# Reordering the second batch of a fused attention and MLP kernel: loads of k, q, v and the weights, and the order of up units and head pairs

## The chip, the cores and the metric

The kernel runs on one core of one Trainium2 chip. The metric is the device time of one execution in microseconds (us), smaller is better; a time is given as a median over several runs. The core has five engines, each working through its own list of instructions in order: TensorE (PE; PEld are its weight loads), VectorE (DVE), ScalarE (ACT), GpSimd (POOL) and SyncE (SP). TensorE writes into PSUM banks; the other engines read them. Transfers between the chip's main memory and the on-chip memory run on 16 DMA engines; here SP issues most of them (a hardware queue), and POOL issues those that also convert float32 to bfloat16 (a software queue).

## What is computed

Attention with a sliding window of 128 and a distance bias, 8 batches, 8 heads, 576 tokens, head size 64; its output, as 4608 tokens of 512, goes through an MLP with a hard-swish.

```python
def _attn_ref(q, k, v):
    B, H, S, D = q.shape
    scores = scale * np.matmul(q, k.transpose(0, 1, 3, 2))
    rel = pos[:, None] - pos[None, :]
    bias = slopes[:, None, None] * (-np.abs(rel).astype(np.float32))[None, :, :]
    mask = (rel >= 0) & (rel < 128)
    scores = np.where(mask, scores + bias[None], -1000000000.0)
    scores = scores - np.max(scores, axis=-1, keepdims=True)
    attn = np.exp(scores)
    attn = attn / (np.sum(attn, axis=-1, keepdims=True) + 1e-09)
    return np.matmul(attn, v).astype(np.float32)

def _moe_ref(x, w_in, w_out):          # x: 4608 x 512, w_in: 512 x 2048, w_out: 2048 x 512
    h = x @ w_in
    relu6 = np.clip(h + 3.0, 0.0, 6.0)
    g = h * relu6 / 6.0
    return (g @ w_out).astype(np.float32)
```

## The kernel before

**Tiling.** Attention works on pairs of heads: pair `g` has batch `g // 4` and heads `2 * (g % 4)` and the next, so batch 0 has pairs 0 to 3 and batch 1 pairs 4 to 7. The MLP works on tiles of 512 tokens, nine in all. One *up unit* (`moe_up`) is one block of 128 of the 2048 hidden columns for one tile of tokens: four matmuls of 512 columns (`up_mms`), then ACT's `r6` (line 524) and DVE's product (line 525) into `gbuf`. One *down step* (`moe_down`, lines 553 to 556) is four matmuls towards a block of 128 output rows. `units` holds all of these in their order, and `fill(n)` takes the next n of them; it stops before an up unit whose tokens are not attended yet (`done`).

**The order is written by hand.** The whole body stands under a manual schedule of all five engines, so each engine gets its instructions exactly in the order in which the Python code calls them. `first_batch` does the attention of batch 0, `second_batch` that of batch 1 among the 16 up units of token tile 0, and `segment` all the rest; the change touches `second_batch` and the last lines of `first_batch` ahead of `attend_split(0, ...)`.

**Steps of the second batch.**
- `load_double(b, dp, nm)` asks for k or q of four heads (two pairs, `dp` 0 or 1) in two loads of 288 KB into the left or right half of `ldbuf[1]` (k) or `ldbuf[0]` (q). `prepare_double` casts these to bfloat16 in two copies of 128 x 576 on the engines given (`P` POOL, `V` DVE). `wide_double` transposes the result with nine matmuls into a score bank and copies it, 128 x 1152, to `kTb` or `qTb` (line 290).
- `load_heads` and `load_block` ask for v (two heads at a time, and the last 64 tokens of all heads), `cast_heads` and `cast_v` turn these to bfloat16 on POOL (lines 199 and 196).
- `scores_diag(g)` and `scores_off(g)` are the score matmuls; each takes one of two score banks (`ps_sc`). `exp_diag(g, e)` is an exp on ACT and a select on POOL that masks it (line 388); `exp_off_full(g)` is one exp of 1024 columns (line 369).
- `attend(g)` multiplies with v (34 matmuls of 65 columns) into a score bank and normalises on DVE (lines 446 and 447). `back(g)` transposes the result (line 481) and ACT, for pair 7 DVE, copies it to `xT` (line 487).
- `up_begin` and `up_more` do an up unit of token tile 1 in parts, as that needs all four pairs of batch 1.
- `load_w_in(g)` and `load_w_out(g)` are POOL's converting loads of a quarter of the weights (512 columns of w_in, so up units 4g to 4g + 3, or 512 rows of w_out). The first quarter of w_in comes another way, through `load_raw` and `cast_raw`.
- `hold(buf, col)` writes one element of a load buffer on DVE: the load into that buffer that follows in the code has to wait for this write, and so is held back until DVE gets there.

**What sets the order of the transfers.** SP issues its loads in code order. Its completion counters are eight, used in turn, so at most eight of its loads are in flight: the ninth is issued when the first has landed. A load into a buffer waits until the casts that read the buffer's old contents are done.

Of the kernel before, what the change touches and what calls it, by code (L numbers as in the profile page):

```python
# [11 lines left out]
BF16 = mybir.dt.bfloat16  # L12
# [6 lines left out]
def kernel(  # L19
# [76 lines left out]
    def load_double(b, dp, nm, eng):  # L96
        for e in range(2):
            eng.dma_start(out=ldbuf["qk".index(nm)][:, ds((2 * dp + e) * RT * D, RT * D)],
                          in_=src_of[nm][b, ds(4 * dp, 4), :, :].rearrange(
                              "(i e) (a t) d -> e a i (t d)", e=2, t=RT)[e])  # L100
# [12 lines left out]
    def load_heads(b, nm, hp, eng):  # L113
        for e in range(2):
            h = 2 * hp + e
            eng.dma_start(out=tokens(b, nm)[:, 0:4, h, :],
                          in_=src_of[nm][b, h, 0:512, :].rearrange("(j p) d -> p j d", p=128))
# [57 lines left out]
    def load_w_in(g):  # L175
        nc.gpsimd.dma_start(
            out=w_in_sb[:, :, ts(g, 512)],
            in_=moe_w_in[:, ts(g, 512)].rearrange("(k p) f -> p k f", p=128))
# [15 lines left out]
    def cast_v(b, j, copy):  # L194
        n = min(128, S - j * 128)
        copy(out=vbuf[b % 2][:n, j, :, 0:D], in_=ld[b, "v"][:n, j, :, :])

    def cast_heads(b, hp, copy):
        copy(out=vbuf[b % 2][:, 0:4, ds(2 * hp, 2), 0:D], in_=ld[b, "v"][:, 0:4, ds(2 * hp, 2), :])
# [20 lines left out]
    st = {}  # L220
# [8 lines left out]
    def transposes(g, copies):  # L229
        b, hp = divmod(g, NP)  # L230
        for nm, dst, copy in (("q", qTb[b % 2], copies[0]), ("k", kTb[b % 2], copies[1])):
            src = st.pop((g, nm))
            tp = ps_h.tile([128, RT, RP], BF16, tag="h", name="tp", padded_shape=[128, 16, 64])
            for t in range(RT):
                for e in range(2):
                    r = slice(e * D, (e + 1) * D)
                    nc.tensor.transpose(tp[r, t, :], src[r, ts(t, D)], ident[r, r])
            copy(out=dst[:, hp, :, :].rearrange("p j c -> p (j c)")[:, 0:S].rearrange(
                "p (a t) -> p a t", t=RT), in_=tp.rearrange("p t a -> p a t"))

    def prepare_double(b, dp, copies, nms="kq", early=None):
        for nm, copy in zip(nms, copies):
            pr = prs.tile([128, RT, 2 * D], BF16, tag=f"pr{nm}", name="pr2")
            for e in range(2):
                copy(out=pr[:, :, ts(e, D)],  # L245
                     in_=ldbuf["qk".index(nm)][:, ds((2 * dp + e) * RT * D, RT * D)].rearrange(
                         "p (t d) -> p t d", t=RT))
                if early and (nm, e) == (nms[0], 0):
                    early()
            st[b, dp, nm] = pr  # L250
# [117 lines left out]
    def exp_off_full(g):  # L368
        nc.scalar.activation(out=st[g, "po"].rearrange("p e j c -> p e (j c)"),
                             in_=st[g, "sco"], func=ACT.Exp, scale=scale)  # L370
# [206 lines left out]
    def fill(n):  # L577
        for _ in range(n):
            if at[0] == len(units):
                return  # L580
            nt, fn, step = units[at[0]]
            if fn is moe_up and done[0] < NP * (min((nt * NT + NT - 1) // S, B - 1) + 1):
                return
            fn(nt if fn is moe_up else nt - 1, step)
            at[0] += 1
# [26 lines left out]
    def hold(buf, col):  # L612
        nc.vector.memset(ldbuf[buf][:, col:col + 1], 0.0)

    def first_batch():
        prepare(0, (V, A))
        warm_up(5)
        tables_diag(0)
        tables_off(0)
        transposes(0, (V, A))  # L620
        scores_diag(0)
        prepare(1, (P, V))
        nc.gpsimd.memset(ldbuf[2][:, 0:1], 0.0)
        load_heads(0, "v", 0, nc.sync)
        load_block(0, "v", 4, nc.sync)
        load_heads(0, "v", 1, nc.sync)
        load_heads(0, "v", 2, nc.sync)
        load_raw(0)
        load_raw(1)
        load_heads(0, "v", 3, nc.sync)  # L630
        load_raw(2)
        load_raw(3)
        transposes(1, (V, V))
        scores_off(0)
        exp_full(0)
        scores_diag(1)
        prepare_double(0, 1, (V, P), "qk")
        tables_off(1)
        scores_off(1)
        double_begin(0, 1, "q", ("av", "o"))  # L640
        double_begin(0, 1, "k", ("h", "h"))
        exp_full(1)
        double_copy(0, 1, "q", 0, (V, V))
        double_copy(0, 1, "k", 0, (A, A))
        tables_diag(2)
        tables_off(2)
        scores_diag(2)
        double_copy(0, 1, "q", 1, (V, V))
        double_copy(0, 1, "k", 1, (V, V))
        scores_off(2)  # L650
        exp_full(2)
        cast_heads(0, 0, P)
        cast_v(0, 4, P)
        cast_heads(0, 1, P)
        cast_heads(0, 2, P)
        load_w_in(1)
        cast_heads(0, 3, P)
        for ks in range(n_ks):
            cast_raw(ks, P)
        load_w_in(2)  # L660
        attend_split(0, ("av", "o"))
        scores_diag(3)
        attend_split(1, ("h", "h"))
        scores_off(3)
        exp_full(3)
        attend(2)
        hold(1, 0)
        for nm in "kq":
            load_double(1, 0, nm, nc.sync)
        back(0, "av")  # L670
        back(1, "o")
        attend(3)
        back(2, "h")
        up_begin(0, 0, 2)
        back(3, "av")
        up_begin(0, 1, 2, "o")
        up_more(0, 0, 3)
        up_more(0, 1, 3)
        done[0] = NP

    def second_batch():
        memsets_later()
        fill(5)
        hold(3, 0)
        load_heads(1, "v", 0, nc.sync)
        load_block(1, "v", 4, nc.sync)
        load_heads(1, "v", 1, nc.sync)
        for nm in "kq":
            load_double(1, 1, nm, nc.sync)
        for hp in (2, 3):  # L690
            load_heads(1, "v", hp, nc.sync)
        fill(2)
        prepare_double(1, 0, (P, V), "kq")
        load_w_in(3)
        fill(1)
        wide_double(1, 0, "k", V)
        wide_double(1, 0, "q", A)
        for dp in range(1):
            for nm in "kq":
                load_double(2, dp, nm, nc.sync)  # L700
        fill(2)
        g = NP
        scores_diag(g)
        exp_diag(g, 0)
        exp_diag(g, 1)
        fill(1)
        scores_off(g)
        exp_off_full(g)
        scores_diag(g + 1)
        exp_diag(g + 1, 0)  # L710
        exp_diag(g + 1, 1)
        fill(1)
        scores_off(g + 1)
        exp_off_full(g + 1)
        cast_heads(1, 0, P)
        cast_v(1, 4, P)
        cast_heads(1, 1, P)
        fill(1)
        attend(g)
        fill(1)  # L720
        attend(g + 1)
        back(g, "o")
        fill(1)
        prepare_double(1, 1, (P, V), "kq")
        back(g + 1, "o")
        wide_double(1, 1, "k", V)
        wide_double(1, 1, "q", A)
        for nm in "kq":
            load_double(2, 1, nm, nc.sync)
        fill(1)  # L730
        scores_diag(g + 2)
        exp_diag(g + 2, 0)
        exp_diag(g + 2, 1)
        load_w_out(0)
        up_begin(1, 0, 2)
        scores_off(g + 2)
        exp_off_full(g + 2)
        up_begin(1, 1, 2)
        scores(g + 3)
        exp_diag(g + 3, 0)  # L740
        exp_diag(g + 3, 1)
        exp_off_full(g + 3)
        cast_heads(1, 2, P)
        cast_heads(1, 3, P)
        load_w_out(1)
        prepare_double(2, 0, (P, P), "kq")
        load_w_out(2)
        load_w_out(3)
        attend(g + 2)
        attend(g + 3)  # L750
        prepare_double(2, 1, (P, P), "kq")
        nc.gpsimd.memset(ldbuf[2][:, 0:1], 0.0)
        load_tokens(2, "v")
        for dp in range(2):
            load_double(3, dp, "k", nc.sync)
        load_tokens(3, "q")
        back(g + 2)
        up_more(1, 0, 3)
        up_more(1, 1, 3)
        back(g + 3)  # L760
        done[0] = 2 * NP
        fill(4)
        double(2, 0, "k", 0, "av", A)
        fill(1)
        double(2, 0, "k", 1, "av", A)
        fill(1)
        wide_double(2, 0, "q", V)
        fill(4)
        scores_diag(2 * NP)
        scores_off(2 * NP)  # L770
# [94 lines left out]
```

## Time and profile before

| | us |
|---|---|
| median of three runs | 340.91 |
| lowest, highest | 339.87, 341.17 |
| the profiled execution | 340.78 |
| its span, first to last instruction | 339.1 |

| stretch (us) | what runs there |
|---|---|
| 0 to 20.9 | batch 0: constants, loads, attention |
| 20.9 to 27.7 | up units 0 to 7 of token tile 0 |
| 27.7 to 59.5 | batch 1's attention among up units 8 to 15 |
| 59.5 to 75.9 | up units of token tile 1, batch 2's transposes and first scores |
| 75.9 to 339 | down steps, up units and attention interleaved, to the end |

Landing times of loads in this profile, from issue: w_in's second, third and last quarter 8.3, 9.4 and 8.7 us; w_out's quarters 5.7, 5.4, 6.1 and 7.4; k and q of batch 1's first two pairs 4.4 to 7.7; of its second two pairs 4.9 to 5.5; its v 4.4 to 8.1.

A page of the profile has, among other parts, the busy time of each engine, the span in 40 slices with a digit for the busy share in tenths (8.48 us a slice here), and the clock that TensorE was granted. The timeline of an engine lists its instructions with their start and length, and in brackets how long the engine was idle before one and what ended that. In all of these L524 is line 524 of the kernel.

### The profile page before, as it was taken

What the parts mean: (1) busy time and instruction counts of PE and PEld (TensorE: products, weight loads), DVE (VectorE), ACT (ScalarE), POOL (GpSimd) and SP (SyncE); (2) the same over time, 40 slices, a digit from 0 to 9 for tenths busy, and PEclk for the clock granted to TensorE, in tenths of its full rate; (3) what the DMA queues carried; (4) which work ended last, traced back from release to release, by engine and by line L of the source; (5) the groups of instructions that cost most, each with busy time, mean ns of one, the idle gap of its engine ahead of it and who ended that gap; (6) DMA issues with size and microseconds to landing.
All of it is one profiled execution on the core that took longest, in us unless ns stands there. A gap on an engine that the chain in (4) does not pass through costs nothing.

```text
span 339.1 us, 6923 instructions
## 1 busy us (share of the span) xinstructions
PE 318.1 (94%) x2659; PEld 167.7 (49%) x2659; DVE 175.6 (52%) x348; ACT 196.3 (58%) x336; POOL 139.9 (41%) x252
## 2 busy tenths in 40 slices
PE   7997875979997999999999999999999999999996
PEld 4654443434544544554567664555445444444443
DVE  5768543364433556455556555555556555445510
ACT  3876773457656776576667665766657244334411
POOL 5561629007747676636665466554333000000000
PEclk9999997699999999999999999999999999999999
DMA  7999979993599999899989999993211101000112
GB/s 271 220 228 207 256 253 155 195 239 79 120 226 227 204 211 212 193 187 204 235 181 223 194 222 175 215 199 64 59 50 52 50 31 60 36 31 33 49 56 83
DMA packets 131602, 52.43 MB, mean 155 GB/s; under 512 B 119153, under 2 KB 122993, under 8 KB 131569
## 3 DMA queue, kind: packets, MB, share of 16 engines
q1 hardware_dynamic: 126864, 46.41, 64.4%
q0 software_dynamic: 3696, 3.67, 7.2%
q10 hardware_dynamic: 1008, 1.90, 1.5%
q8 instruction: 21, 0.34, 0.5%
q14 instruction: 13, 0.10, 0.1%
HBM read 36.70 MB, written 9.44 MB: 136 GB/s over the span
## 4 chain that ended last, share of the span: by engine, by line
PE 85%; ACT 6%; DVE 4%; DMA 2%; issue 2%; POOL 0%; SPq 0%; DVEq 0%; POOLq 0%; ACTq 0%
PE ops L555 36%; PE hps L500 33%; PE scd L330 3%; DMA ldbuf<-in_q_dram 2%; PE av L425 2%; PE av L417 2%; PE sco L362 2%; ACT r L524 2%; DVE gbuf L525 1%; PE ops L536 1%; PE scd L305 1%; PE tp L260 1%; ACT gbuf L385 1%; ACT xT L487 1%; PE w L163 1%
## 5 line engine op out<-in xcount | busy, mean ns | idle before, releaser
L524 ACT ACTIVATE r<-hps,bias 128x512 f32<-128x512 f32 x144 | 98.9, 689 | 98.3 <-PE hps L500 97.6
L525 DVE SCALAR_TENSOR_TENSOR gbuf<-r,hps 128x512 bf16<-128x512 f32 x144 | 98.5, 687 | 105.4 <-ACT r L524 103.2
L500 PE MATMUL hps<-xT,w_in_sb 128*128 128x512 bf16 (+1 forms) x640 | 147.9, 364 | 4.8 <-DVE gbuf L525 3.3
L555 PE MATMUL ops<-w_out_sb,gbuf 128*128 128x512 bf16 x560 | 137.8, 379 | 1.1 <-DVE osb L564 1.1
L500 PEld LDWEIGHTS <-w_in_sb 128*128 128x128 bf16 x640 | 60.0, 99 | 61.4 <-issue 9.6
L555 PEld LDWEIGHTS <-gbuf 128*128 128x128 bf16 x560 | 52.4, 98 | 58.1 <-issue 1.3
L388 POOL TENSOR_SCALAR_AFFINE_SELECT pd<-pd 128x512 bf16<-128x512 bf16 x48 | 29.5, 631 | 45.4 <-ACT pd L385 45.4
L398 POOL TENSOR_SCALAR_AFFINE_SELECT po<-po 128x512 bf16<-128x512 bf16 x48 | 30.1, 632 | 31.4 <-ACT po L395 31.1
L564 DVE COPY osb<-ops 128x512 f32<-128x512 f32 x33 | 22.7, 688 | 27.8 <-PE ops L555 27.8
L385 ACT ACTIVATE pd<-scd,bias_d 128x512 bf16<-128x512 f32 x48 | 31.3, 683 | 4.7 <-PE scd L330 4.7
L395 ACT ACTIVATE po<-sco,bias_o 128x512 bf16<-128x512 f32 x48 | 33.1, 689 | 0.0
L212 POOL CAST tbuf<-ldbuf 128x512 bf16<-128x512 f32 (+1 forms) x45 | 25.5, 611 | 16.6 <-issue 11.8
L436 DVE TENSOR_TENSOR avs<-av,rc 128x384 bf16<-128x384 f32 (+1 forms) x48 | 23.6, 491 | 1.7
L417 PE MATMUL av<-vbuf,po 128*128 128x65 bf16 x192 | 18.1, 193 | 0.9 <-DVE avs L436 0.9
L425 PEld LDWEIGHTS <-pd 128*128 128x128 bf16 x192 | 14.3, 97 | 7.7 <-issue 0.5
L425 PE MATMUL av<-vbuf,pd 128*128 128x65 bf16 x192 | 17.5, 194 | 0.0
L417 PEld LDWEIGHTS <-po 128*128 128x128 bf16 x192 | 14.3, 98 | 3.5 <-DVE avs L436 1.0
L401 ACT ACTIVATE p4buf<-sco,bias_d 128x64 bf16<-128x64 f32 x48 | 15.6, 324 | 0.0
L330 PE MATMUL scd<-qTb,kTb 64*128 64x128 bf16 x256 | 13.0, 222 | 1.1 <-DVE pr L226 0.7
L330 PEld LDWEIGHTS <-kTb 64*128 64x128 bf16 x256 | 7.6, 96 | 13.0 <-issue 9.2
L245 POOL CAST pr<-ldbuf 128x576 bf16<-128x576 f32 x18 | 11.5, 667 | 4.7 <-DMA ldbuf<-in_k_dram 2.4
L205 POOL CAST vbuf<-ldbuf 128x1024 bf16<-128x1024 f32 x12 | 12.1, 1040 | 0.0
(107 smaller groups left out, 222.2 us busy)
## 6 DMA issues: line engine op xcount, KB each, us to landing
out_dram<-osb SPq DMA_DIRECT2D x33, 256.0 KB, 2.5
ldbuf<-in_v_dram SPq DMA_DIRECT2D x24, 256.0 KB, 4.5
ldbuf<-in_q_dram SPq DMA_DIRECT2D x20, 256.0 KB, 4.7
ldbuf<-in_k_dram SPq DMA_DIRECT2D x16, 256.0 KB, 4.8
ldbuf<-in_q_dram SPq DMA_DIRECT2D x12, 288.0 KB, 5.0
ldbuf<-in_k_dram SPq DMA_DIRECT2D x12, 288.0 KB, 4.8
ldbuf<-in_v_dram SPq DMA_DIRECT2D x24, 128.0 KB, 4.6
w_out_sb<-in_moe_w_out_dram POOLq DMA_DIRECT2D x4, 512.0 KB, 5.9
```

Source lines behind the costliest of these rows:

```text
L212: nc.gpsimd.tensor_copy(out=tbuf[:m, :, j, :], in_=s[:m, j, :, :].rearrange("p (i e) d -> p i (e d)", e=2))
L330: nc.tensor.matmul(scd[:, e, ts(j, 128)], lhsT=kT[r, j, :], rhs=qT[r, j, :], start=first, stop=first or j == 3)
L385: nc.scalar.activation(out=pd[:, e, :, :].rearrange("p j c -> p (j c)"), in_=sc[:, e, :], func=ACT.Exp, bias=bias_d[:, h:h + 1], scale=scale)
L388: nc.gpsimd.affine_select(out=pd[:, e, :, :], in_=pd[:, e, :, :], pattern=[[0, 4], [1, 128]], channel_multiplier=-1, base=0, compare_op=AL ...
L395: nc.scalar.activation(out=po[:, e, :, :].rearrange("p j c -> p (j c)"), in_=sc[:, e, :], func=ACT.Exp, bias=bias_o[:, h:h + 1], scale=scale)
L398: nc.gpsimd.affine_select(out=po[:, e, :, :], in_=po[:, e, :, :], pattern=[[0, 4], [-1, 128]], channel_multiplier=1, base=-1, compare_op=A ...
L417: nc.tensor.matmul(out_av, lhsT=po[:, e, qt % 4, :], rhs=vb[:, qt - 1, h, :], start=True, stop=False)
L425: nc.tensor.matmul(out_av, lhsT=d, rhs=vb[:, qt, h, :], start=(qt == 0), stop=True)
L500: nc.tensor.matmul(hps[:, lo:hi], lhsT=w_in_sb[:, ks, ts(ms, 128)], rhs=xT[:, ks, ds(src, hi - lo)], start=(ks == 0), stop=(ks == n_ks - 1))
L524: nc.scalar.activation(out=r6, in_=hps, func=ACT.Relu, bias=bias3[:, 0:1], scale=1.0 / 6.0)
L525: nc.vector.scalar_tensor_tensor(out=gts[nt][:, ms, :], in0=r6, scalar=1.0, in1=hps, op0=ALU.min, op1=ALU.mult)
L555: nc.tensor.matmul(ops[nt, sub], lhsT=gts[nt][:, ms, ts(sub, 128)], rhs=w_out_sb[:, ms, :], start=(ms == 0), stop=(ms == n_ms - 1))
```

## The change

In `first_batch`, w_in's third quarter is no longer asked for behind `cast_raw`. In `second_batch`:
- the first double's k is cast on POOL in two halves by a new helper, `prepare_half`, at the head of the batch; w_in's third quarter is asked for between the halves, its last one behind them;
- a POOL write of one element of `ldbuf[1]` stands behind these casts, and so holds the second double's k (and with SP's order q and v) until then; DVE's `hold(3, 0)` goes; SP asks for the second k and q ahead of all v instead of in the middle of it;
- batch 2's first k and q are asked for before instead of behind the first wide transposes;
- the second double's casts and transposes move from behind the attends of pairs 4 and 5 into the scores of pairs 4 and 5;
- pair 6's scores come ahead of the attends of 4 and 5, pair 7's between them; v's casts on POOL all stand behind pair 6's diagonal scores; the attends of 4 and 5, their `back`s, and the scores of 6 and 7 now lie among the last up units of token tile 0, and the half units of tile 1 (`up_begin`) behind both `back`s instead of among pair 6's and 7's scores;
- w_out's first quarter is asked for behind the first v casts, its second behind the last v casts, which stand ahead of pair 7's selects.

```diff
+    def prepare_half(b, dp, nm, e, copy):
+        if e == 0:
+            st[b, dp, nm] = prs.tile([128, RT, 2 * D], BF16, tag=f"pr{nm}", name="pr2")
+        copy(out=st[b, dp, nm][:, :, ts(e, D)],
+             in_=ldbuf["qk".index(nm)][:, ds((2 * dp + e) * RT * D, RT * D)].rearrange(
+                 "p (t d) -> p t d", t=RT))
...
             cast_raw(ks, P)
-        load_w_in(2)
         attend_split(0, ("av", "o"))
...
     def second_batch():
         memsets_later()
-        fill(5)
-        hold(3, 0)
+        prepare_half(1, 0, "k", 0, P)
+        load_w_in(2)
+        prepare_half(1, 0, "k", 1, P)
+        nc.gpsimd.memset(ldbuf[1][:, ds(2 * RT * D, 1)], 0.0)
+        load_w_in(3)
+        for nm in "kq":
+            load_double(1, 1, nm, nc.sync)
         load_heads(1, "v", 0, nc.sync)
         load_block(1, "v", 4, nc.sync)
-        load_heads(1, "v", 1, nc.sync)
+        for hp in (1, 2, 3):
+            load_heads(1, "v", hp, nc.sync)
+        fill(7)
+        prepare_double(1, 0, (V,), "q")
+        fill(1)
         for nm in "kq":
-            load_double(1, 1, nm, nc.sync)
-        for hp in (2, 3):
-            load_heads(1, "v", hp, nc.sync)
-        fill(2)
-        prepare_double(1, 0, (P, V), "kq")
-        load_w_in(3)
-        fill(1)
+            load_double(2, 0, nm, nc.sync)
         wide_double(1, 0, "k", V)
         wide_double(1, 0, "q", A)
-        for dp in range(1):
-            for nm in "kq":
-                load_double(2, dp, nm, nc.sync)
-        fill(2)
+        fill(1)
         g = NP
         scores_diag(g)
         exp_diag(g, 0)
@@
         fill(1)
         scores_off(g)
         exp_off_full(g)
+        fill(1)
         scores_diag(g + 1)
+        prepare_double(1, 1, (P,), "k")
         exp_diag(g + 1, 0)
         exp_diag(g + 1, 1)
         fill(1)
+        prepare_double(1, 1, (V,), "q")
+        for nm in "kq":
+            load_double(2, 1, nm, nc.sync)
         scores_off(g + 1)
         exp_off_full(g + 1)
+        wide_double(1, 1, "k", V)
+        wide_double(1, 1, "q", A)
+        fill(1)
+        scores_diag(g + 2)
+        exp_diag(g + 2, 0)
+        exp_diag(g + 2, 1)
         cast_heads(1, 0, P)
         cast_v(1, 4, P)
         cast_heads(1, 1, P)
-        fill(1)
-        attend(g)
-        fill(1)
-        attend(g + 1)
-        back(g, "o")
-        fill(1)
-        prepare_double(1, 1, (P, V), "kq")
-        back(g + 1, "o")
-        wide_double(1, 1, "k", V)
-        wide_double(1, 1, "q", A)
-        for nm in "kq":
-            load_double(2, 1, nm, nc.sync)
-        fill(1)
-        scores_diag(g + 2)
-        exp_diag(g + 2, 0)
-        exp_diag(g + 2, 1)
         load_w_out(0)
-        up_begin(1, 0, 2)
+        fill(1)
         scores_off(g + 2)
         exp_off_full(g + 2)
-        up_begin(1, 1, 2)
+        cast_heads(1, 2, P)
+        cast_heads(1, 3, P)
+        load_w_out(1)
+        attend(g)
+        fill(1)
         scores(g + 3)
         exp_diag(g + 3, 0)
         exp_diag(g + 3, 1)
         exp_off_full(g + 3)
-        cast_heads(1, 2, P)
-        cast_heads(1, 3, P)
-        load_w_out(1)
+        attend(g + 1)
+        back(g, "o")
+        fill(1)
+        back(g + 1, "o")
+        up_begin(1, 0, 2)
+        up_begin(1, 1, 2)
         prepare_double(2, 0, (P, P), "kq")
```

More of the change, by code (lines that the diff above doesn't have):

```diff
@@ L712, in second_batch @@
         fill(1)
+        prepare_double(1, 1, (V,), "q")
+        for nm in "kq":
+            load_double(2, 1, nm, nc.sync)
         scores_off(g + 1)
         exp_off_full(g + 1)
-        cast_heads(1, 0, P)
-        cast_v(1, 4, P)
-        cast_heads(1, 1, P)
-        fill(1)
-        attend(g)
-        fill(1)
-        attend(g + 1)
-        back(g, "o")
-        fill(1)
-        prepare_double(1, 1, (P, V), "kq")
-        back(g + 1, "o")
         wide_double(1, 1, "k", V)
         wide_double(1, 1, "q", A)
-        for nm in "kq":
-            load_double(2, 1, nm, nc.sync)
         fill(1)
@@ L733, in second_batch @@
         exp_diag(g + 2, 1)
+        cast_heads(1, 0, P)
+        cast_v(1, 4, P)
+        cast_heads(1, 1, P)
         load_w_out(0)
-        up_begin(1, 0, 2)
+        fill(1)
         scores_off(g + 2)
         exp_off_full(g + 2)
-        up_begin(1, 1, 2)
+        cast_heads(1, 2, P)
[3 more added lines that the diff above has]
+        fill(1)
         scores(g + 3)
```

## The prediction

> **What bounds the kernel now.** I read the page first, then the TensorE timeline of the second batch (27 to 76 us), then the waits that end its gaps, then POOL's and SP's queues and the landing times, and last the granted clock in windows of 3.41 us.
>
> ```profile
> span 339.1 us, 6923 instructions
> PE 318.1 (94%) x2659; PEld 167.7 (49%) x2659; DVE 175.6 (52%) x348; ACT 196.3 (58%) x336; POOL 139.9 (41%) x252
> ...
> PE   7997875979997999999999999999999999999996
> ...
> PEclk9999997699999999999999999999999999999999
> ```
>
> TensorE is the bound (94%). Its only long thin stretch after the start is slices 3 to 8 (26 to 76 us), which are the steps that the change reorders; there too the granted clock falls. After 76 us TensorE is nearly full, and nothing there is edited. So the answer is how far the start of the first down-projection (75.94 us now) moves.
>
> ```profile
> 27.65 0.67 PE L288 MATMUL tp<-ident,pr 128*128 128x128 bf16 x9
> 30.01 0.68 PE L288 MATMUL tp<-ident,pr 128*128 128x128 bf16 x9 [1.70 <-DVE pr L245]
> 30.53 1.89 PE L500 MATMUL hps<-xT,w_in_sb 128*128 128x512 bf16 x8
> ...
> 38.27 0.22 PE L425 MATMUL wide<-vbuf,gbuf 128*128 128x65 bf16 x2 [0.53 <-POOL vbuf L199]
> ```
>
> Start, length, form; in brackets the gap and what ended it. The same view has gaps of 1.65 us at 45.03 (q's second transposes, on DVE casts), 1.51 at 52.17 (attend of pair 6, on POOL's v cast), and 0.61, 0.73, 0.55, 1.14 between 54.06 and 59.48 (the last attends, transposes and half units).
>
> ```profile
> 51.69:55.10 3.41, 1.73 (x41) 1.49 (x41) 2.00 (x4) 0.62 (x2) 3.41 (x6) 1.00 0.99 156
> 55.10:65.34 10.24, 8.41 (x29) 3.58 (x29) 3.11 (x5) 3.38 (x7) 4.74 (x9) 0.50 1.12 179
> 65.34:68.75 3.41, 3.26 (x25) 1.78 (x24) 2.14 (x3) 2.54 (x4) 0.00 (x0) 1.00 0.99 208
> 41.45:44.86 3.41, 1.66 (x18) 0.88 (x15) 2.78 (x5) 1.84 (x3) 0.00 (x0) 1.00 0.95 315
> 27.79:31.21 3.42, 1.72 (x23) 1.20 (x21) 3.23 (x5) 1.17 (x2) 0.00 (x0) 1.00 1.15 183
> ```
>
> Columns: stretch, its length, busy PE, PEld, DVE, ACT, POOL, granted clock, DMA share, GB/s. The clock is 0.50 for 10.24 us, three times 3.41. The 3.41 us ahead of the fall have 1.73 us of busy TensorE, but no 512-column matmul: 34 attend matmuls of 65 columns and 5 transposes of 128, some 2850 columns. Two other windows of the same grid, no busier (1.66 and 1.72), kept the full clock with 3100 to 3700 columns, by my count. I take some 2900 to 3100 columns per window as the edge.
>
> **The change part by part.** No arithmetic is added or removed; one POOL memset (0.10 us) is added, one DVE memset (0.06) removed. I laid out the second batch instruction by instruction in both orders, each engine in its own order, with durations from rows: an up unit 0.86 us on TensorE (4 x 0.216), nine transposes 0.56, an attend 0.57, r6 0.60, one diagonal exp 0.59, an off exp 0.92 on ACT, a product 0.62, an SBUF cast 0.66, a wide copy 1.27 on DVE, a select 0.58, a v cast 0.56, a k cast 0.61, a DMA issue 0.75 on POOL. For the old order at full clock this puts the first whole unit of tile 1 at 58.58, against 59.48 measured, where the half clock from 55.1 is in the difference. The order's gaps on TensorE sum to 12.1 us. Now the new order.
>
> *First q, k.* The third quarter of w_in no longer runs beside q's load, whose second half landed at 29.16 (21.44 + 7.7). But DVE reaches the q casts only after the product that ends at 28.27, in both orders: 28.27 + 2 x 0.66 + 0.1 = 29.7 instead of 30.01. Gain 0.3 us, no more.
>
> *Third quarter of w_in.* It is asked for behind the first k cast instead of ahead of the memsets, and the ninth up unit (columns 1024 on) reads it.
>
> ```profile
> 20.99 0.74 POOL L176 DMA_DIRECT2D w_in_sb<-in_moe_w_in_dram  x1
> ...
> 24.08 0.66 POOL L245 CAST pr<-ldbuf 128x576 bf16<-128x576 f32 x1 [1.21 <-DMA ldbuf<-in_k_dram]
> ```
>
> Now it lands at 20.99 + 9.4 = 30.4, just ahead of that unit (30.53). In the new order it is issued at 24.08 + 0.61 = 24.7, as k's first half landed before this quarter's bytes began. Alone, the nearest row is the first quarter of w_out, 5.7 us from issue to landing: 30.4. Beside other loads the w_in rows have 8.7 and 9.4: 33.4 to 34.1. Between them: POOL's new memset releases k, q of the second double at 26.2, and SP's loads show bytes some 1.95 us after issue (19.54 to 21.5), so at 28.15; w_out's bytes come at full rate 2.3 us after issue (49.28 to 51.55), 0.188 MB/us alone (0.47 MB in 51.5 to 54.0), and software-queue loads get 0.097 beside others (0.29 MB in 25 to 28). That is 0.22 MB by 28.15, the other 0.30 by 31.3, landing 31.3 to 31.8. I take 31.5. The unit could start at 30.26, so TensorE waits 1.3 us (bounds 0.1 and 3.8). Behind it in TensorE's queue stand pair 4's scores; ACT's exps and POOL's selects wait for these.
>
> The Trainium skill (DMA: Bandwidth & Descriptors, Anatomy of one DMA) fits a POOL-issued DMA with 2.0 us plus bytes over 436 GB/s; for the 1 MiB read that gives an estimate of 4.4 us, a landing at 29.1 and no wait, 1.3 us less than my sum. The 5.7 us row speaks against it.
>
> *Second k, q.* They land by some 35 us in the new order (7.7 us after issues up to 28.1, the worst q row); POOL casts k after pair 4's selects (34.6). q's casts stand on DVE behind the twelfth product, and that behind pair 5's exps on ACT: q's transposes wait 2.1 us instead of 1.67 in the layout of the old order, and those of k 0.6 for pair 5's exps to free the score bank, in place of two waits of 0.13 and 0.34.
>
> *v.* Its loads now follow k, q on SP; SP keeps eight in flight, so the last goes out near 36.5 and, at 4.4 to 8.1 us, lands by 44.6, against its cast at 46.6 or later: hidden, and a cover of 2 us. But attend of pair 4 now stands right behind pair 6's selects and the v casts on POOL: gap 1.1 instead of 0.8 (0.53 in the trace).
>
> *Last units.* The 1.6 us wait of pair 6's attend for v, 0.4 for a score bank, 0.9 of waits at the earlier backs, all go; new are 1.0 ahead of the half units (they now stand behind the copies of pair 4's and 5's x), 0.9 at pair 5's attend (pair 7's exps hold the bank) and 0.3 of small ones. The four gaps of the tail stay.
>
> *w_out, and k, q of batch 2.* w_out's first two quarters are asked for earlier by 2 to 5 us, and are read from 75.94: nothing. If POOL were late, one issue costs 0.75, which here is hidden under exps. k, q of batch 2 go out behind v, from some 37 us, land before 50, and are cast at 49.7 and later. POOL ends this stage 3 to 4 us sooner, so batch 2's v is asked for sooner.
>
> Sum: the new gaps are 13.06 us against 12.12, with the same work: +0.94, of which the late quarter is 1.3. On the profiled execution, 340.78 us (span 339.1 and 1.7 around it), this gives 341.7. The median shown, 340.91, is 0.13 above that execution: 341.9, if one fall of the clock stays, as now. Then the first down-projection starts at 76.9.
>
> **The rivals.**
> 1. *A second fall of the clock, at the new wait.* Between the k transposes (27.65) and the late unit (31.5) there are 18 transposes only, 2300 columns in 3.9 us, under the 2850 that preceded the fall at 55.1; on the old grid, 27.79 to 31.21 is such a window. Half rate for one window or more costs up to half of 3.41 us, as TensorE is then back to back to 37 us: 341.9 + 1.7 = 343.6, and 344.9 with the later landings. This is the slower side; it decides from a landing after some 30.8. Against it: the grid's place in another execution isn't shown, and a window must fall on these 3.9 us.
> 2. *The fall at 55.1 goes.* Two half units of 512 columns (0.86 us) now stand right ahead of the last two attends, so the window that tripped can hold 2000 columns more. The fall's price: laid out at full clock, the old order starts the down-projection at 72.85 instead of 75.94, 3.1 us (half of the 8.41 busy us, 4.2, less what waits swallow). 341.9 - 3.1 = 338.8; a shorter fall 340. Against it: the tail's gaps are unchanged, and later windows are as thin. The Trainium skill (TensorE: Matmul & The Clock Gate, What's actually happening) has the clock halved after an idle window of some 3.4 us. By that rule neither the new wait nor the tail would trip it, which is this rival; the trace's fall after a window 51% busy speaks against the rule.
> 3. *The quarter is in time* (landing at 30.4). Then the reordering is an exchange of waits, -0.2 us: 340.7. For it: q's load is out of the way by 27.
>
> **How the numbers follow.** Forecast 0.42, own range 340.7 to 343.2; rival 1 0.22, rival 2 0.22, rival 3 0.14. About 0.5% (1.7 us) is what a measurement of this kernel can tell from no change: faster under 339.2, slower over 342.6. Faster: 0.22 of rival 2 and 0.03 of rival 3, 0.25. Slower: rival 1 whole, 0.16 of the forecast (a landing past 32.2) and 0.01: 0.39. The rest, 0.36, is within. The range over all is 338.4 to 344.9: rival 2's 338.8 with 0.4 for the layout's error, rival 1 with a late landing.
>
> **What would show it.** The ninth up unit starting at 31 to 32 behind a wait on w_in's DMA (right), or at 30.3 (rival 3). q's second transposes after a gap near 2 us; no long wait of pair 6's attend; a clock row with 0.5 near 31 to 35 (rival 1), or none at 55 to 65 (rival 2). The sum is wrong if the down-projection starts outside 75 to 78 us, or if the stretch behind it, unedited, changes its length by over 1 us.

## The result, and the profile after

| | before | changed |
|---|---|---|
| median of 10 runs each, us | 340.45 | 339.18 |
| lowest, highest | 339.67, 341.64 | 337.92, 339.97 |
| ratio, 95% interval | | 0.9955 (0.9933 to 0.9976) |
| profiled execution: time, span | 340.78, 339.1 | 339.23, 337.5 |
| its first down-projection starts | 75.94 | 74.22 |
| its time at half clock | 10.2 | 6.8 |

The change makes the kernel faster: by 1.3 us in the medians, by 0.45% as the ratio has it. The forecast was 341.9, slower by 1.0. The unedited part behind 76 us kept its length (339.1 - 75.94 = 263.2; 337.5 - 74.22 = 263.3), so in these two executions the whole difference arose in the stretch that was laid out. Below, six of the 77 runs of the kernel before that were taken beside the experiments, each over 1.5% above its fastest and with the lowest clocks (0.973 or 0.974), are left out.

The page of the changed kernel, busy share of TensorE and granted clock in 40 slices:

```profile
span 337.5 us, 6920 instructions
...
PE   7987785979997999999999999999999999999996
...
PEclk9999899799999999999999999999999999999999
```

Slices of 8.4 us. Before, the clock row has 7 and 6 side by side; now it has 8 in the slice from 34 to 42 us and 7 in that from 59 to 67: two falls apart from each other instead of one long one. TensorE's timeline of the changed kernel (start, length, form, gap and what ended it):

```profile
29.43 0.68 PE L295 MATMUL tp<-ident,pr 128*128 128x128 bf16 x9 [1.42 <-DVE pr L252]
29.94 1.03 PE L507 MATMUL hps<-xT,w_in_sb 128*128 128x512 bf16 x4
...
38.98 1.14 PE L295 MATMUL tp<-ident,pr 128*128 128x128 bf16 x9 [1.88 <-DVE pr L252]
...
54.33 0.45 PE L488 MATMUL tb<-ident,avs 128*128 128x128 bf16 x5 [0.62 <-DVE avs L454]
55.51 0.59 PE L507 MATMUL hps<-xT,w_in_sb 128*128 128x512 bf16 x2 [0.73 <-ACT xT L494]
...
56.92 0.59 PE L507 MATMUL hps<-xT,w_in_sb 128*128 128x512 bf16 x2 [0.55 <-DVE xT L494]
58.87 3.01 PE L507 MATMUL hps<-xT,w_in_sb 128*128 128x512 bf16 x8 [1.35 <-DVE gbuf L532]
```

The ninth up unit (29.94) has no bracket: it starts right behind q's transposes, and the wait of 1.3 us that I forecast is absent. The other gaps are near the layout: q's second transposes 1.88 (laid out 2.1), the tail as before.

Why the third quarter of w_in was in time: POOL issued it at 24.16 and it landed 5.3 us later, at 29.5. The DMA queues of the changed kernel, first in 26.4 to 29.0 us, then in 29.0 to 32.0 (q0 is POOL's software queue, q1 SP's hardware queue; packets, MB, share of the 16 engines):

```profile
q0 software_dynamic: 492, 0.49, 117.8%
```

```profile
q0 software_dynamic: 275, 0.27, 61.2%
q1 hardware_dynamic: 191, 0.41, 41.3%
```

The first answer has no line for q1 at all. SP had issued the second k at 25.64, but no byte of it moved up to 29.0, while 0.49 MB of the software queue went through, at 0.188 MB/us. My estimate had the quarter share the engines from 28.15 on.

The granted clock, in windows laid on the falls of the changed kernel (stretch, length, busy PE, PEld, DVE, ACT, POOL, clock, DMA share, GB/s):

```profile
35.50:38.95 3.45, 1.59 (x24) 1.01 (x22) 2.47 (x5) 2.29 (x4) 1.22 (x2) 1.00 0.96 181
38.95:42.36 3.41, 3.38 (x22) 1.79 (x23) 1.24 (x1) 1.62 (x2) 0.00 (x0) 0.51 0.99 236
42.36:45.80 3.44, 2.55 (x38) 1.67 (x38) 1.37 (x2) 2.85 (x5) 2.61 (x5) 0.99 0.98 330
56.00:59.40 3.40, 1.50 (x11) 0.73 (x10) 1.73 (x3) 1.27 (x2) 0.31 (x2) 1.00 1.15 162
59.40:62.80 3.40, 3.40 (x14) 1.56 (x12) 0.87 (x3) 1.57 (x3) 0.00 (x0) 0.51 1.11 212
62.80:66.20 3.40, 3.37 (x25) 1.74 (x23) 1.84 (x4) 2.30 (x4) 0.00 (x0) 0.99 1.04 224
```

Each fall follows a window with less than half of TensorE busy (1.59 and 1.50), and each lasts one window, as TensorE is full in it (3.38 and 3.40). The same view of the kernel before, in its one fall:

```profile
55.10:58.51 3.41, 2.56 (x9) 1.08 (x9) 0.46 (x1) 0.64 (x2) 3.41 (x6) 0.50 1.06 163
58.51:61.93 3.42, 2.45 (x6) 0.84 (x6) 1.28 (x2) 1.25 (x3) 1.33 (x4) 0.50 1.11 156
61.93:65.34 3.41, 3.41 (x15) 1.66 (x14) 1.37 (x2) 1.48 (x4) 0.00 (x0) 0.50 1.18 219
```

There TensorE had gaps in the first two windows (2.56, 2.45) though it ran at half rate, and the clock came back only after the third, which was full.

The windows lie elsewhere in each execution, and with them the falls. A second profile of the same changed kernel (its run beside the experiments) has one fall only:

```profile
35.88:39.29 3.41, 1.53 (x28) 1.07 (x26) 2.43 (x5) 1.95 (x3) 1.17 (x2) 1.00 1.20 204
39.29:42.70 3.41, 3.19 (x21) 1.53 (x20) 1.16 (x2) 2.13 (x3) 0.00 (x0) 0.50 1.02 251
56.36:59.77 3.41, 1.67 (x7) 0.67 (x7) 1.62 (x3) 1.28 (x3) 0.00 (x0) 1.00 1.11 160
59.77:63.18 3.41, 3.05 (x22) 1.63 (x21) 1.49 (x3) 2.91 (x5) 0.00 (x0) 1.00 1.09 208
```

The 13 kept traces (the two kernels and the 11 runs below), each cut into windows of 3.41 us at the times where its clock steps, have 15 falls up to the last matmul. Each follows a window with 1.16 to 1.77 us of busy TensorE, but seven windows with 1.46 to 1.78 kept the full clock, so thinness alone doesn't decide whether the clock falls; what else does is open. What ends a fall is the same in all 20 windows at half clock: behind the 15 with TensorE busy for 3.11 us or more the clock came back, behind the five with 1.92 to 2.56 it did not.

### The profile page after: what moved, and what is told of

The parts are those of the page before. It is cut to its first block, busy times and chain, and to the rows that moved or that the text cites. A ratio compares the mean times of both kernels' runs of the same rounds, so it can differ in the third digit from the quotient of the medians.

```text
span 337.5 us, 6920 instructions
## 1 busy us (share of the span) xinstructions
PE 315.5 (93%) x2659; PEld 166.3 (49%) x2659; DVE 176.0 (52%) x347; ACT 196.5 (58%) x336; POOL 139.7 (41%) x253
## 4 chain that ended last, share of the span: by engine, by line
PE 82%; ACT 5%; DMA 4%; DVE 3%; SPq 2%; issue 1%; POOL 1%; DVEq 0%; POOLq 0%
PE hps L507 36%; PE ops L562 35%; PE scd L337 2%; PE av L432 2%; ACT r L531 2%; PE av L424 2%; PE sco L369 1%; DMA ldbuf<-in_q_dram 1%; SPq L116 1%; DMA ldbuf<-in_v_dram 1%; DMA xT<-avs 1%; PE ops L543 1%; DVE gbuf L532 1%; ACT gbuf L392 1%; PE tp L267 1%
## 5 line engine op out<-in xcount | busy, mean ns | idle before, releaser
L395 POOL TENSOR_SCALAR_AFFINE_SELECT pd<-pd 128x512 bf16<-128x512 bf16 x48 | 29.5, 631 | 47.8 <-ACT pd L392 47.8
L405 POOL TENSOR_SCALAR_AFFINE_SELECT po<-po 128x512 bf16<-128x512 bf16 x48 | 30.1, 632 | 31.6 <-ACT po L402 31.3
L392 ACT ACTIVATE pd<-scd,bias_d 128x512 bf16<-128x512 f32 x48 | 31.3, 683 | 4.7 <-PE scd L337 4.7
L337 PEld LDWEIGHTS <-kTb 64*128 64x128 bf16 x256 | 7.3, 95 | 13.7 <-issue 10.2
L442 DVE RECIPROCAL rc<-av 128x6 f32<-128x6 f32 (+1 forms) x48 | 8.8, 183 | 5.6 <-PE av L432 5.6
```

Of the source, the lines that this page charges most:

```text
L337: nc.tensor.matmul(scd[:, e, ts(j, 128)], lhsT=kT[r, j, :], rhs=qT[r, j, :], start=first, stop=first or j == 3)
L392: nc.scalar.activation(out=pd[:, e, :, :].rearrange("p j c -> p (j c)"), in_=sc[:, e, :], func=ACT.Exp, bias=bias_d[:, h:h + 1], scale=scale)
L395: nc.gpsimd.affine_select(out=pd[:, e, :, :], in_=pd[:, e, :, :], pattern=[[0, 4], [1, 128]], channel_multiplier=-1, base=0, compare_op=AL ...
L405: nc.gpsimd.affine_select(out=po[:, e, :, :], in_=po[:, e, :, :], pattern=[[0, 4], [-1, 128]], channel_multiplier=1, base=-1, compare_op=A ...
```

## The experiments

Theory A: the two orders take the same time at full clock, and the gain is that fewer windows of 3.41 us run at half clock. Theory B: the gain is in the order, or in the loads, and the clock is a by-product. Every run comes with its mean granted clock, from which the number of windows at half clock follows: (1 - clock) x 2 x span / 3.41, rounded to whole windows (what is over is mostly half clock behind the last matmul, 0.67 us in the profile of the kernel before). The kernel before ran along with each set of experiments, so ratios are against runs on the same chip.

**Spare matmuls in the gaps of both orders.** `warm_up(n)` is the kernel's own helper: n matmuls of 512 columns from the identity, read by nobody. In the changed kernel:

```diff
         wide_double(1, 1, "k", V)
+        warm_up(7)
         wide_double(1, 1, "q", A)
...
+        warm_up(3)
         attend(g)
...
+        warm_up(2)
         back(g + 2)
+        warm_up(3)
         up_more(1, 0, 3)
         up_more(1, 1, 3)
         back(g + 3)
+        warm_up(2)
         done[0] = 2 * NP
-        fill(4)
+        fill(2)
+        warm_up(5)
+        fill(2)
```

> The changed kernel with spare matmuls of 512 columns on the attend bank that nobody reads, put into TensorE's long gaps of the second batch (7 ahead of q's second transposes, 3 ahead of pair 4's attend, 2, 3, 2 and 5 around the last transposes and half units). They leave the order and all loads as they are. Theory A (the change gains by the clock: it falls for 6.8 us in its profile instead of 10.2, and at full clock both orders take the same): no row under 1.00 between 26 and 76 us, the first down-projection near 72.5 us instead of 74.2, and 337.3 us, within 0.5 of the old order with spare matmuls. Theory B (the gain is in the order of the steps, the clock is a by-product): this kernel stays 1.3 us under the old order with spare matmuls.

In the kernel before, 6 ahead of q's second transposes, 5 ahead of `attend(g + 2)`, and the same tail:

> The kernel before with the same kind of spare matmuls in its own gaps (6 ahead of q's second transposes, 5 ahead of pair 6's attend, 2, 3, 2 and 5 around the last transposes and half units). Theory A: the clock stays up, the first down-projection at 72.9 instead of 75.9 us (the layout at full clock), 337.4 us, so the old order gains more from them (3.0 us) than the new one (1.9) and the two end within 0.5 us of each other. Theory B: it ends at 338.5 or more, 1.3 us above the changed kernel with spare matmuls.

Measured: the changed order 337.86 us, ratio to before 0.9929 (0.9901 to 0.9956); the old order 338.45, 0.9931 (0.9906 to 0.9956). The two intervals lie on each other. The clock row of the old order with spare matmuls:

```profile
span 336.7 us, 6930 instructions
...
PEclk9999999999999999999999999999999999999999
```

No fall is left; its first down-projection starts at 72.99 us, laid out 72.9. That of the changed order starts at 72.50. Runs without a window at half clock had a mean of 337.4 (6 runs, changed order) and 337.7 (6 runs, old order). The other six runs of each order still had one window (one run of the old order two); in the profile of the changed order it lies at 105 to 109 us, behind two gaps of 0.9 us near 102 and 104. So each kernel got 4 more spare matmuls at either place, ahead of pair 11's `values(g - 1, (3, 4))` and between the two score parts of pair 13:

> The changed kernel with all spare matmuls of its first version, and 4 more at each of two thin places near 102 and 104 us (ahead of pair 11's last values and between the two score parts of pair 13), where 6 of 12 runs of that version still had one window at half clock. Theory A (only the windows at half clock separate the kernels): no such window in most runs, 337.3 us (the runs of the first version that had none lay at 337.1 to 337.7), and within 0.5 us of the old order with the same additions. Theory B: 1.3 us under the old order with the same additions.

> The kernel before with its spare matmuls and the same 8 more near 102 and 104 us. Theory A: no window at half clock in most runs and 337.5 us, 0.2 above the new order with the same (the layout's difference of the two orders at full clock when w_in's third quarter is in time). Theory B: 338.6 us or more.

Measured: 337.37 us, 0.9902 (0.9882 to 0.9923), and 337.51, 0.9906 (0.9887 to 0.9925), with 1 of 12 runs having a window at half clock. With the clock kept up the old order is as fast as the new one, to 0.14 us in the medians. Theory A holds, and theory B's 1.3 us between them is not there.

**The same without spare matmuls, by counting.** The changed kernel was run again beside the other experiments:

> The changed kernel itself, on the chip and in the rounds of the three others, so that they are compared with it directly, with the clock of each run. Both theories: near 339.2 us (338.0 to 340.0), with the clock at 0.5 for about two windows of 3.41 us where the kernel before has three or four, and 1.0 us for each window.

339.50 us, 0.9964 (0.993 to 0.9998). The runs of the two unaltered kernels with the clock recorded, sorted by windows at half clock (mean us, runs):

| windows | before | changed |
|---|---|---|
| 1 | 338.4 (1) | 338.2 (6) |
| 2 | 339.4 (9) | 339.5 (13) |
| 3 | 340.5 (30) | 340.3 (3) |
| 4 | 341.6 (30) | none |
| 5 | 343.1 (1) | none |
| mean number | 3.3 (71) | 1.9 (22) |

At an equal number of windows the kernels are within 0.2 us of each other. Straight lines through the single runs give 1.1 us for each window in both kernels, and 337.3 (before) and 337.2 us (changed) with none, near the 337.5 and 337.4 of the runs with spare matmuls. The changed kernel has 1.4 windows fewer: 1.4 x 1.1 = 1.5 us, against 1.3 and 1.4 in the medians. So the gain is the windows; that the changed order has fewer of them because its thin windows have full ones behind them is read from the profiles, in which the falls near 55 us of the old order lasted three windows (two traces of two) and those near 59 of the new order one (four of five).

**One thin place at a time.** The changed kernel with only the first two groups of spare matmuls, and with only those of the tail:

> The changed kernel with spare matmuls only ahead of q's second transposes (7) and of pair 4's attend (3), none in the tail. Theory A (each window at half clock costs about 1 us, the order at full clock is not the gain): the fall at 39 us goes, the one near 59 us stays in most runs, and the time lies about 1 us under the changed kernel, near 338.2. If the fall at 39 us costs nothing as waits behind it swallow it: as the changed kernel.

> The changed kernel with spare matmuls only in the tail (2, 3, 2 and 5 around the last transposes and half units, 54 to 59 us), none at 37 to 45 us. Theory A with about 1.1 us for each window: the windows near 59 us go, the one near 39 us stays where the grid meets the 1.9 us gap, and the time lies between the changed kernel (339.5) and the one with both (337.9), near 338.7.

338.84 us, 0.9933 (0.9903 to 0.9963), with 1.4 windows a run; and 337.20, 0.9905 (0.9884 to 0.9926), with 0.5. The first moved as expected by sign (0.7 of the 1.3 us). The second was better than expected, as good as all of them together. Its set ran on another chip than the first, on which the kernel before took 340.6 instead of 340.9; by ratios the tail is worth more than the middle, but these two intervals overlap.

**Loads without order, order without loads.** First the changed loads and first k casts with the old order of the rest (`second_batch` of the changed kernel down to the first `wide_double`, then that of the kernel before), then the reverse:

> The changed kernel's loads and first k casts (third quarter of w_in between the k casts, the hold on POOL, second k and q ahead of v) with the old order of scores, attends, second transposes and up units. If the loads carry the gain: 339.2 us, as the changed kernel. If the order of the steps and with it the clock carries it: q's first transposes come 0.3 us sooner as DVE finds q landed, all else as before, 340.1 us, and the clock falls near 55 us for three windows as before.

> The old loads and first casts (third quarter of w_in behind the raw casts, DVE's hold, second k and q behind v's first loads) with the new order of scores, attends, transposes and up units. If the loads are only there to serve the order: second k and q land at 38 to 40 us, their casts wait for them, q's second transposes come some 2 us later than in the changed kernel (at 41 instead of 39), and the run takes 340.5 to 341.5 us. If the order alone carries the gain: 339.2 us.

The loads alone: 343.52 us, 1.0103 (1.0064 to 1.0142), slower than either expectation, with 4.4 windows at half clock in the mean. Its TensorE timeline:

```profile
37.29 1.04 PE L507 MATMUL hps<-xT,w_in_sb 128*128 128x512 bf16 x3 [1.06 <-DMA w_in_sb<-in_moe_w_in_dram]
...
40.02 0.22 PE L432 MATMUL wide<-vbuf,gbuf 128*128 128x65 bf16 x2 [1.69 <-POOL vbuf L199]
```

The old order needs w_in's last quarter at 36 us, and it lands 11.4 us after its issue at 25.86, as second k and q share the engines with it; and it needs v's first heads at 38, which are now behind k and q. I had named neither. In the changed order the unit that reads the last quarter starts at 39.9, and attend at 45.0.

The order alone: 341.44 us, 1.0021 (0.9995 to 1.0046), in the range expected if the loads are there to serve the order. Its timeline, at q's second transposes and those of k ahead of them:

```profile
38.44 0.68 PE L288 MATMUL tp<-ident,pr 128*128 128x128 bf16 x9 [1.43 <-POOL pr L245]
40.14 0.68 PE L288 MATMUL tp<-ident,pr 128*128 128x128 bf16 x9 [1.03 <-DVE pr L245]
```

A new wait for the k casts, which wait for k's landing: 1.2 us lost against the changed kernel (40.14, not 38.98), and 2.7 windows at half clock in the mean. So neither half of the change is a gain by itself.

**The place of w_in's third quarter.** Back where it was, and then, with all else as changed, behind the second k cast and the hold:

```diff
         prepare_half(1, 0, "k", 0, P)
-        load_w_in(2)
         prepare_half(1, 0, "k", 1, P)
         nc.gpsimd.memset(ldbuf[1][:, ds(2 * RT * D, 1)], 0.0)
+        load_w_in(2)
         load_w_in(3)
```

> The changed kernel with w_in's third quarter back where it was, behind the raw casts: it then shares the engines with batch 1's first q, whose second half lands near 29 us instead of 25. If q's landing was hidden anyway behind DVE's products (my prediction): q's first transposes come 0.3 us later, the time is 339.2 to 339.6, as the changed kernel. If the place of the quarter was worth the gain: 340.4 us, as before.

> The changed kernel with w_in's third quarter asked for behind the second k cast and POOL's hold instead of between the casts, 0.7 to 0.9 us later and behind the release of SP's loads of the second k and q. Theory S (software and hardware queue share the DMA engines as I reckoned in the prediction, so what counts is only the issue time): it lands 0.8 us later, near 30.3 us, the ninth up unit waits 0.3 us, and the time is within 0.5 us of the changed kernel. Theory F (whichever queue's packets are there first holds the engines: the second k's bytes came only when the quarter's were through): here k and q go first, the quarter takes 8.5 us or more and lands at 33 or later, the ninth unit waits 3 us or more, the clock falls there, and the run takes 342 us or more.

Early: 339.67 us, 0.9968 (0.9938 to 0.9999), the same as the changed kernel beside it (339.50). q's first transposes have the same gap, 1.42 us: q's landing is hidden behind DVE's products either way, and the new place of the quarter is not what gains.

Later: 343.54 us, 1.0076 (1.0046 to 1.0106), 4.0 us over the changed kernel. The ninth unit in its timeline:

```profile
32.09 0.82 PE L507 MATMUL hps<-xT,w_in_sb 128*128 128x512 bf16 x3 [1.83 <-DMA w_in_sb<-in_moe_w_in_dram]
```

The quarter took 6.8 us from 25.25 instead of 5.3 from 24.16. Here SP issued the second k at 25.34, beside it, and the queues in 26.4 to 29.0 us show both moving:

```profile
q0 software_dynamic: 145, 0.15, 46.5%
q1 hardware_dynamic: 118, 0.27, 32.4%
```

That is the sharing that I had reckoned with for the changed kernel. Landing (32.05) and wait (1.83) are between the two expectations, nearer to theory F's 33 and 3, and the total is F's. The fall of the clock that theory F has at this wait is not in the profile (an execution of 340.72 us, the fastest of the twelve, with its two windows at half clock at 57.59 to 64.42):

```profile
26.87:30.29 3.42, 1.97 (x22) 1.26 (x20) 3.15 (x6) 1.30 (x2) 0.00 (x0) 1.00 0.99 201
30.29:33.70 3.41, 1.46 (x13) 0.73 (x15) 1.10 (x1) 1.66 (x2) 0.00 (x0) 1.00 1.14 288
```

The twelve runs have 3.3 windows in the mean, 1.5 more than the changed kernel beside them; where the others fell is not known. Of the 4.0 us, 1.5 x 1.1 are clock and some 1.8 the wait, with some 0.5 left over that no run explains. So the third quarter has a slack of about half a microsecond in the changed kernel, and POOL's hold is what keeps second k and q behind it in the profiles.

## Why the prediction was wrong

- **The bound and the stretch: right in the profiles shown.** Only the steps between 26 and 76 us moved the time there, and TensorE's own waits count. In other runs a window at half clock near 105 us, behind unedited steps, comes on top.
- **The layout of both orders at full clock: right.** It put the first down-projection at 72.85 us in the old order; with the clock held up it starts at 72.99 and 72.30 in two executions. Without a late quarter the reordering was an exchange of waits worth -0.2 us; measured are -0.14 and -0.3, too small to be told from none.
- **The third quarter's landing: the first step that failed.** "Landing 31.3 to 31.8. I take 31.5" and the wait of 1.3 us. It was 29.46, no wait. Of the 2.7 us between forecast and result this is 1.3. Half a microsecond of the error in the landing is the issue, at 24.16 instead of 24.7, as k's first half had landed sooner. The rest of the term was built on two readings. That SP's loads show bytes 1.95 us after issue (19.54 to 21.5) was no latency alone: until 21.5 the software queue's load of w_in's second quarter filled the engines, and in the changed kernel the interval is over 3.4 us (25.64 to past 29.0), until the third quarter is through. And the contended rate of 0.097 MB/us came from a stretch in which hardware loads had been issued first (k and q's first half at 19.54 to 20.80, the quarter at 20.99). The lower bound that I kept, the lone load's 5.7 us, was the right row. The rule of the Trainium skill that I set against it (DMA: Bandwidth & Descriptors, Anatomy of one DMA), an estimate of 4.4 us for the load, also said no wait, and so did better than my sum; the trace has 5.3 us.
- **"If one fall of the clock stays, as now": the second step that failed, and the one that holds the gain.** I priced the fall as one event of 3.1 us that either stays or goes, from one profile, with "a shorter fall 340" only as an aside in rival 2. It is a number of windows that differs from run to run, 3.3 before and 1.9 after in the mean, at about 1.1 us each: the 1.5 us of gain, and the rest of the distance to the forecast. Rival 2 had the place and the sign, but not that two short falls could stand for one long one: I looked at what precedes a fall, and not at what ends it. A fall before lasted three windows with two thin ones in it; the changed order has full windows behind its thin ones. Nor does the edge of 2900 to 3100 columns a window hold, which I took from one profile: in the changed order with spare matmuls the window ahead of the fall at 105 us has some 4000, by the same count.
- **Rival 1: its condition didn't arise, and its mechanism is not shown.** With the quarter made late the run took 343.54, against the 343.6 that rival 1 gave, but the one profile of it kept the full clock at the wait (1.46 us busy in 30.29 to 33.70), so the agreement of the numbers may be luck. Rival 3's condition came true, but its 340.7 left the clock out.
- **Second q, v, last units: sizes right.** The gap at q's second transposes is 1.88 (2.1 laid out), at pair 4's attend 0.89 (1.1), at pair 5's 0.68 (0.9), ahead of the half units 0.61 (1.0).
- **The rule of the Trainium skill on the clock** (TensorE: Matmul & The Clock Gate, What's actually happening) asks for an idle window ahead of a fall. All falls seen here followed windows with 1.16 to 1.77 us of busy TensorE; the measurement decides against the rule as I read it.

## What to carry to other kernels

Where TensorE is the bound and has thin stretches, count windows at half clock over many runs before pricing a reorder: here the order was worth 0.1 to 0.3 us at full clock, and the clock 1.1 us for each window, and 31 spare matmuls in the gaps of the old order (337.5 us, 0.9906 of before) gained more than the reorder. What ends a fall counts as much as what starts it: here it was always a window in which TensorE was busy for 3.1 of 3.41 us or more, so a thin stretch should have a full one behind it. Where a weight load and other loads meet, the one issued first by 1.5 us can have the engines to itself, as here, and its slack can be half a microsecond.

## What the runs showed that was not expected

- A hardware-queue load issued 1.5 us behind a software-queue load of 512 KB moved no byte while that ran (25.64 to 29.0 us); issued at the same time, the two shared the engines (0.27 and 0.15 MB in 2.6 us). What decides between the two was not tried further.
- The changed kernel with spare matmuls only in its tail, 12 in all, took 337.20 us, 0.9905 of before, and is with the two fullest versions (337.37 and 337.51) the fastest seen; the three are not told apart by these runs.
